# Routing counts in a fused attention, MLP and expert kernel: indicators in blocks of six token tiles, and two token tiles to one counting product in the six-bit rounds

## The chip, the cores and the metric

One core of a Trainium2 chip runs the whole program. The metric is the device time of one execution in microseconds; the time before is the median of three runs, 1070.74 us (1070.49 to 1074.46).

## The reference, cut to what matters

Chunked attention and an MLP produce one row of 512 numbers for each of 3072 tokens. The last part routes these rows to eight experts with a capacity of 384 tokens each, in the order of all 24576 logits, and sends each token through its expert:

```python
def _moe2_ref(x, w_gate, w1, w2) -> np.ndarray:
    N, D = x.shape
    E = w_gate.shape[1]
    cap = N // E
    logits = x @ w_gate
    flat = logits.flatten()
    order = np.argsort(-flat)
    ...
    for idx in order:
        tok, e = (int(idx) // E, int(idx) % E)
        if assigned[tok] >= 0 or counts[e] >= cap:
            continue
        assigned[tok] = e
        counts[e] += 1
    ...
    for e in range(E):
        mask = assigned == e
        h = np.maximum(x[mask] @ w1[e], 0.0)
        out[mask] = h @ w2[e]
    return out.astype(np.float32)
```

## The kernel before, in words

**Tokens and phases.** The 3072 tokens are 24 tiles of 128 (`T = 24`). The greedy assignment is done in eight phases: each phase finds the logit at which the next expert is full, assigns what lies above it, closes that expert and starts again. `route(ph)` (L810) does a phase. What it finds, `eid[ph]` (which expert) and `ids[ph]` (its 384 tokens, made in `listing`, L906), lets the expert's weights be fetched (`fetch`, L950) and its token rows be gathered (`gather`, L991).

**The search for the threshold.** A token's best logit is turned into an integer key of 32 bits, and the threshold is found digit by digit, from the top, in five rounds: `RB = ((25, 7), (18, 7), (12, 6), (6, 6), (0, 6))`, two rounds with digits of seven bits (128 values) and three with six bits (64 values). In a round VectorE builds indicators (`indicate`, L737): for each token and each digit value n, whether the token's digit is at least n, in bf16, in two buffers of 12 token tiles each (`NH = 2`, `HT = 12`). A token tile's 128 columns of digit values stand 12 elements apart, since the buffer is ordered by digit value and then by tile; the rounds of six bits fill 64 of the 128 columns. TensorE counts (L829 to L832): one product `first` times `q2` puts in the starting counts, and then there is one product for each of the 24 tiles, which loads the tile's 128 indicator columns as weights and streams the 8 columns of `oh` (which expert each token wants):

```python
pc = psa[0].tile([P, E], F32, tag="pa", name=f"pc{ph}_{r}")
matmul(0.05, pc, first, q2, start=True, stop=False)
for t in range(T):
    matmul(0.047, pc, ind[t // HT][:, :, t % HT], oh[:, :, t], start=False, stop=(t == T - 1))
```

VectorE reads the counts `pc` with a scan (L835), TensorE turns the result into the digit in one product `pb` (L838), and VectorE subtracts it from all keys (L843) before the next round's indicators. A phase thus has five round trips between VectorE and TensorE; the last phase needs none. That makes 35 rounds, 14 with seven bits and 21 with six.

**What runs beside it.** Phase 0 is routed at the end of the MLP: TensorE fills its pauses with products that were kept back for it, the late products (`late_`, L358, lines 346). When the last of them is done, VectorE makes the last tile of token rows (`finish`, L371 to L373) and GpSimd stores it; the gather of phase 0 on GpSimd's queue stands behind that store. Phases 1 to 6 are routed while TensorE runs the experts of the phase before: `ffn1` (products `pf`, 96 of 384 columns) and `ffn2` (products `pg`, 72 of 512 columns). The expert weights land in a ring of four buffers, ScalarE rounds each piece (`e_0`), and VectorE subtracts to get the remainder (`e_1`, in `second`, L972), after which the ring buffer takes the next piece.

**What sets the order.** PE, VectorE and ScalarE run in the order in which the Python code emits the instructions. A planner (`run`, L776) emits them: each piece of work is a generator that yields the engine it wants, a due time and a rank, `clk` holds the time that the planner books for each engine, and the products of `experts()` or `late()` fill TensorE until a piece falls due. A lower rank goes first on an engine: the chain of routing has rank 0 for counts and digits, its VectorE work rank 1 in phases 0 and 1 and rank 3 later, and `second` rank 2 from the third half-expert on.

**Names in the rows.** Buffers of the attention are used again: `vw` holds indicators, `kwin`, `qk`, `wk` and `kT` hold keys, masks and small tables, `o` is a late product's output, `x` a tile of token rows, `x2d` their store in memory, `xg` the gathered rows, `px` their transposes, `xgh` and `xgl` the two parts of these, `raws` the ring. All VectorE calls of the router have line 582 and all its products line 761, since helpers emit them.

## Time and profile before

| what | before |
|---|---|
| median of three runs | 1070.74 us |
| profiled execution: its time, its span | 1072.39 us, 1070.6 us |
| TensorE busy (matmul), share of the span | 1010.0 us, 94% |
| VectorE busy, share | 793.8 us, 74% |
| ScalarE busy, share | 460.7 us, 43% |
| GpSimd busy, share | 204.7 us, 19% |
| counting products with indicator weights (`pc`) | 840, 204 ns each from start to end |
| mean granted TensorE clock | 0.984 of full |

Busy time of TensorE counts from a product's start to its modelled end, and products overlap: the counting products are 204 ns long but start closer together than that. So a stage in which TensorE shows no idle time is read by the starts of its products and not by its busy share. The profile's slices show four stages: attention and MLP to about 683 us, the routing of phase 0 under the late products to 716 us, a gap with little on TensorE to about 735 us, and eight experts to the end.

### The profile page before, as it was taken

The numbers are of one execution on the slowest core, as the hardware profiler recorded it, in microseconds if no ns is written. First come the engines' busy times: TensorE is split into PE (matmuls) and PEld (weight loads), VectorE is DVE, ScalarE is ACT, GpSimd is POOL, SyncE is SP. The second block draws the span as 40 slices with busy tenths as digits, with TensorE's granted clock in tenths as the row PEclk, the third lists the DMA queues.
The fourth block names the chain that finished last, engine by engine and source line by source line (L and its number), as shares of the span: only waits on it lengthen the run. The fifth ranks groups of instructions, "written<-read, shape, count | busy, mean of one in ns | idle before, by whom it ended". The sixth has DMA issues, their size and how long they took to land.

```text
span 1070.6 us, 24583 instructions
## 1 busy us (share of the span) xinstructions
PE 1010.0 (94%) x9397; PEld 888.7 (83%) x9397; DVE 793.8 (74%) x2879; ACT 460.7 (43%) x991; POOL 204.7 (19%) x227
## 2 busy tenths in 40 slices
PE   4668899999999999999999999987999999999997
PEld 3647688888988889888888889866898988988996
DVE  4999864986698969898969854376968769678720
ACT  3666554444444544445444445312414334233621
POOL 2566540000021101021101000001103202032211
PEclk9989999999999999999999999996999999999999
DMA  6966504221212121212121100032624426235600
GB/s 158 230 184 185 148 19 128 58 58 38 58 38 59 39 58 38 57 39 59 38 58 39 38 2 2 20 117 91 197 92 145 130 88 208 88 140 176 227 30 30
DMA packets 140373, 96.52 MB, mean 90 GB/s; under 512 B 99288, under 2 KB 123864, under 8 KB 140128
## 3 DMA queue, kind: packets, MB, share of 16 engines
q1 hardware_dynamic: 135968, 81.32, 27.1%
q0 software_dynamic: 4000, 13.11, 3.4%
q8 instruction: 74, 1.21, 0.5%
q10 hardware_dynamic: 288, 0.52, 0.1%
q14 instruction: 43, 0.35, 0.1%
HBM read 82.33 MB, written 12.60 MB: 89 GB/s over the span
## 4 chain that ended last, share of the span: by engine, by line
PE 72%; DVE 14%; issue 6%; DMA 4%; ACT 1%; POOL 1%; SPq 1%; POOLq 0%; DVEq 0%; ACTq 0%
PE o L346 20%; PE ph L316 20%; PE pf L761 11%; PE pg L761 9%; DVE lsc L387 5%; PE pc L761 5%; DVE u L280 2%; DVE y L281 1%; DVE g L325 1%; PE po L221 1%; DMA xg<-x2d,vw 1%; PE sc L195 1%; PE px L1014 1%; DMA raw<-in_moe_w_out_dram 1%; DMA k<-in_k_dram 1%
## 5 line engine op out<-in xcount | busy, mean ns | idle before, releaser
L316 PE MATMUL ph<-xT,win 128*128 128x256 f32 x2304 | 321.9, 288 | 9.7 <-ACT win L262 6.9
L316 PEld LDWEIGHTS ph<-xT,win 128*128 128x128 f32 x2304 | 300.0, 192 | 27.5 <-ACT win L262 10.3
L346 PE MATMUL o<-wout,g 128*128 128x512 f32 x1038 | 275.3, 401 | 5.2 <-DVE g L325 2.2
L346 PEld LDWEIGHTS o<-wout,g 128*128 128x128 f32 x1038 | 185.1, 190 | 39.7 <-DVE g L325 3.1
L387 DVE SCALAR_TENSOR_TENSOR lsc<-x,wgb 128x128 int8<-128x128 f32 x640 | 158.2, 298 | 3.3 <-DMA wgb<-wgd 1.2
L320 ACT ACTIVATE r<-ph 128x256 f32<-128x256 f32 x192 | 72.7, 381 | 166.5 <-PE ph L316 155.8
L761 PE MATMUL pf<-xgh,e 128*128 128x384 f32 x512 | 137.9, 345 | 0.0
L761 PE MATMUL pg<-e,hh 128*128 128x512 f32 x384 | 124.3, 399 | 0.0
L325 DVE TENSOR_TENSOR g<-r,g 128x256 fp32r<-128x256 f32 x173 | 80.7, 468 | 53.3 <-ACT g L324 50.5
L387 DVE SCALAR_TENSOR_TENSOR lsc<-c,wgb 128x512 int8<-128x512 f32 x128 | 99.1, 774 | 2.1
L761 PEld LDWEIGHTS pf<-xgh,e 128*128 128x128 f32 x512 | 94.0, 192 | 0.4 <-ACT xgh L765 0.2
L761 PE MATMUL pf<-xgl,e 128*128 128x384 f32 x256 | 88.3, 345 | 0.3 <-DVE xgl L582 0.3
L765 ACT ACTIVATE hh<-pf 128x384 fp32r<-128x384 f32 x64 | 31.5, 492 | 129.1 <-PE pf L761 87.0
L765 ACT ACTIVATE e<-raws 128x1024 fp32r<-128x1024 f32 x64 | 65.7, 1056 | 45.5 <-DMA raws<-in_moe_w_dram 45.4
L321 ACT ACTIVATE r<-r 128x256 f32<-128x256 f32 x192 | 79.6, 417 | 5.5
L761 PEld LDWEIGHTS pg<-e,hh 128*128 128x128 f32 x384 | 71.1, 189 | 12.5
L582 DVE TENSOR_TENSOR e<-raws,e 128x1024 fp32r<-128x1024 f32 x64 | 76.8, 1218 | 3.9 <-ACT e L765 3.0
L761 PE MATMUL pg<-e,hl 128*128 128x512 f32 x192 | 75.8, 395 | 0.0
L324 ACT ACTIVATE g<-r 128x256 fp32r<-128x256 f32 x173 | 71.7, 417 | 5.0 <-PE o L346 0.3
L994 POOL DMA_INDIRECT xg<-x2d,vw x24 | 34.8, 1451 | 151.8 <-issue 118.2
L761 PE MATMUL pc<-kwin,vw 128*128 128x8 bf16 x840 | 56.2, 204 | 7.3 <-DVE vw L582 7.3
L582 DVE SCALAR_TENSOR_TENSOR hl<-pf,hh 128x384 fp32r<-128x384 f32 x64 | 35.1, 551 | 35.6 <-ACT hh L765 35.6
(171 smaller groups left out, 1276.7 us busy)
## 6 DMA issues: line engine op xcount, KB each, us to landing
raws<-in_moe_w_dram SPq DMA_DIRECT2D x64, 512.0 KB
vw<-in_v_dram SPq DMA_DIRECT2D x176, 56.0 KB
raw<-in_moe_w_in_dram SPq DMA_DIRECT2D x16, 512.0 KB
raw<-in_moe_w_out_dram SPq DMA_DIRECT2D x16, 512.0 KB
k<-in_k_dram SPq DMA_DIRECT2D x24, 256.0 KB
q<-in_q_dram SPq DMA_DIRECT2D x24, 256.0 KB
x2d<-x SPq DMA_DIRECT2D x20, 256.0 KB
wgb<-wgd SPq DMA_DIRECT2D x1, 2048.0 KB
```

The source lines that it names most:

```text
L280: nc.vector.scalar_tensor_tensor(u, yi, 3, u, op0=ALU.logical_shift_left, op1=ALU.bitwise_or)
L316: nc.tensor.matmul(ph, win_ap(a, kk, f), x[:, kk, :], start=(n == 0), stop=(n == 3 * KD - 1))
L320: nc.scalar.activation(r, ph, AF.Relu)
L321: nc.scalar.activation(r, r, AF.Square)
L324: nc.scalar.activation(hi, r, AF.Copy)
L325: nc.vector.tensor_tensor(lo, r, hi.bitcast(F32), op=ALU.subtract)
L346: nc.tensor.matmul(PO[j][u], g[:, u * P:(u + 1) * P], wout_ap(a, f), start=(f == 0 and n == 0), stop=(f == FT - 1 and n == 2))
L387: nc.vector.scalar_tensor_tensor(sc[:, z], a[:, z], 1.0, b[:, z], op0=ALU.mult, op1=ALU.mult, accum_out=acc[:, i:i + 1])
L582: return getattr(nc.vector, name)(out, *args, **kw)
L761: return nc.tensor.matmul(*args, **kw)
L765: nc.scalar.activation(out, in_, func)
L994: nc.gpsimd.indirect_dma_start(out=xg[:, j, :], out_offset=None, in_=x2d[:, :], in_offset=bass.IndirectOffsetOnAxis(ap=ids[ph][:, j:j + 1] ...
```

## The change

**Layout.** An indicator buffer is ordered by block of six token tiles, then digit value, then tile in the block (`blocks`). A tile's columns then stand 6 elements apart instead of 12, and in a round of six bits the 64 columns of a tile in one block and the 64 columns of the tile in the next block lie at one step behind each other.

**Counting.** In the rounds of six bits one product takes both: 128 weight columns of two tiles against 16 columns, the 8 of `oh` for each. Of the four quarters of its output two mean something: digit values of the first tile with its own 8 columns (partitions 0 to 63, columns 0 to 7), and those of the second (partitions 64 to 127, columns 8 to 15). VectorE copies the second quarter to partitions 0 to 63, adds the first, and scans the sum on 64 partitions; `pb` is made from 64 partitions. A round of six bits has 13 products instead of 25; a round of seven bits keeps its 25.

**VectorE's pieces.** In phases 0 and 1 each block's indicators are an instruction of their own, four to a round instead of two. The remainders of the first three half-experts are made in half pieces (`second`). **Ranks and due times.** VectorE's routing work from phase 2 on has rank 2 instead of 3, and the counting products of a six-bit round fall due 0.3 us later against the indicators than those of a seven-bit round.

```diff
-    q2 = b0.tile([P, E], BF16, name="q2")
+    q2 = b0.tile([P, 2 * E], BF16, name="q2")
...
     def indicators(n):
-        return [sp.tile([P, P, HT], BF16, tag=f"ind{g}", name=f"ind{n}_{g}") for g in range(NH)]
+        return [sp.tile([P, HT // TB, P * TB], BF16, tag=f"ind{g}", name=f"ind{n}_{g}")
+                .rearrange("p k m -> p (k m)") for g in range(NH)]
+
+    def blocks(ind, n):
+        return ind[:, :HT * n].rearrange("p (k n b) -> p k n b", n=n, b=TB)
...
     def indicate(ind, de, g, r):
-        n, z = 2 ** RB[r][1], [P, 2 ** RB[r][1], HT // TB, TB]
-        V.tensor_tensor(ind[:, :n, :].rearrange("p n (a b) -> p n a b", b=TB),
-                        de[:, g * HT:(g + 1) * HT].rearrange("p (a b) -> p a b", b=TB)[:, None].to_broadcast(z),
-                        tabs[r][:, :, None, :].to_broadcast(z), op=ALU.is_ge)
+        n, k = 2 ** RB[r][1], HT // TB
+        z = [P, k, n, TB]
+        V.tensor_tensor(blocks(ind, n),
+                        de[:, g * HT:(g + 1) * HT].rearrange("p (a b) -> p a b", b=TB)[:, :, None, :].to_broadcast(z),
+                        tabs[r][:, None, :, :].to_broadcast(z), op=ALU.is_ge)
...
-        rank = 1 if ph < 2 else 3
+        rank = 1 if ph < 2 else 2
...
-                    indicate(ind[g], de, g, r)
-                yield "pe", V_PE - 0.5 + sl, 0
-                pc = psa[0].tile([P, E], F32, tag="pa", name=f"pc{ph}_{r}")
-                matmul(0.05, pc, first, q2, start=True, stop=False)
-                for t in range(T):
-                    matmul(0.047, pc, ind[t // HT][:, :, t % HT], oh[:, :, t], start=False, stop=(t == T - 1))
+                    if ph > 1:
+                        indicate(ind[g], de, g, r)
+                    else:
+                        n = 2 ** RB[r][1]
+                        for k in range(HT // TB):
+                            V.tensor_tensor(blocks(ind[g], n)[:, k], de[:, None, g * HT + k * TB:g * HT + (k + 1) * TB]
+                                            .to_broadcast([P, n, TB]), tabs[r], op=ALU.is_ge)
+                yield "pe", V_PE - (0.5 if RB[r][1] == 7 else 0.2) + sl, 0
+                n = 2 ** RB[r][1]
+                k = P // n
+                pc = psa[0].tile([P, k * E], F32, tag="pa", name=f"pc{ph}_{r}")
+                matmul(0.05, pc, first, q2[:, 0:k * E], start=True, stop=False)
+                for g in range(T // (k * TB)):
+                    x = ind[g * k * TB // HT].rearrange("p (m b) -> p m b", b=TB)[:, g * k * TB % HT // TB * n:, :]
+                    y = oh[:, :, g * k * TB:(g + 1) * k * TB].rearrange("p e (k b) -> p b k e", b=TB)
+                    for b in range(TB):
+                        matmul(0.047, pc, x[:, 0:P, b], y[:, b], start=False, stop=(g + 1) * k * TB + b == T + TB - 1)
                 yield "v", PE_V, 0
                 fl = small([P, E], BF16, "fl")
-                V.tensor_tensor_scan(fl, pc, ones[:, 0:E], 0.0, op0=ALU.max, op1=ALU.min)
+                if k > 1:
+                    ab = small([P, E], F32, "ab")
+                    V.tensor_copy(ab[0:n], pc[n:P, E:2 * E])
+                    V.tensor_tensor(ab[0:n], pc[0:n, 0:E], ab[0:n], op=ALU.add)
+                V.tensor_tensor_scan(fl[0:n], ab[0:n] if k > 1 else pc, ones[0:n, 0:E], 0.0, op0=ALU.max, op1=ALU.min)
                 yield "pe", V_PE + sl / 2, 0
                 pb = psa[0].tile([P, 2], F32, tag="pa", name=f"pb{ph}_{r}")
-                matmul(0.05, pb, steps[r], fl[:, E - 2:E], start=True, stop=True)
+                matmul(0.05, pb, steps[r][0:n], fl[0:n, E - 2:E], start=True, stop=True)
...
         def second(hi, lo, raw):
-            yield "v", A_V, rank
-            V.tensor_tensor(lo, raw, hi.bitcast(F32), op=ALU.subtract)
+            m = raw.shape[1]
+            k = m // 2 if h < 3 else m
+            for z in range(0, m, k):
+                yield "v", A_V if z == 0 else 0.0, rank
+                V.tensor_tensor(lo[:, z:z + k], raw[:, z:z + k], hi[:, z:z + k].bitcast(F32), op=ALU.subtract)
```

**What it moves.** The planner's times change, so the order of all three engines changes from the routing of phase 0 on. On TensorE, at the end of phase 0's routing, before (`pi` makes the token list of phase 0, `o` are late products, `kT` is the weight of the first counting product of phase 1):

```order
L761 MATMUL pi_10270<-rounded 128x26 x3
L346 MATMUL o_1_9965<-wout_81,k_9785 128x512
L346 MATMUL o_1_9965<-wout_79,k_9785 128x512 x2
L346 MATMUL o_1_9965<-wout_81,k_9785 128x512
L346 MATMUL o_1_9965<-wout_79,k_9785 128x512 x2
L346 MATMUL o_1_9965<-wout_81,k_9785 128x512
L346 MATMUL o_1_9965<-wout_79,k_9785 128x512 x2
L346 MATMUL o_1_9965<-wout_81,k_9785 128x512
L346 MATMUL o_1_9965<-wout_79,k_9785 128x512 x2
L346 MATMUL o_1_9965<-wout_81,k_9785 128x512
L346 MATMUL o_1_9965<-wout_79,k_9785 128x512
L761 LDWEIGHTS kT_9685
```

With the change, the same stretch:

```order
L767 MATMUL pi_10258<-rounded 128x26 x3
L346 MATMUL o_1_9965<-wout_79,k_9785 128x512 x2
L346 MATMUL o_1_9965<-wout_81,k_9785 128x512
L346 MATMUL o_1_9965<-wout_79,k_9785 128x512
L767 LDWEIGHTS kT_9685
```

Behind `pi` stood 14 late products (a row with x2 is two), and 4 stand there now; the ten others have gone in front of it, between the rounds of phase 0.

On VectorE, a little later, before (`x_23` is the last tile of token rows, `kwin_0` and `vw_0` keys and indicators of phase 1):

```order
L582 TENSOR_TENSOR kwin_0_9681<-kwin_0_9681,kT_9685 128x120
L582 TENSOR_TENSOR vw_0_9679<-kwin_0_9681,qk_9684 128x24
L582 TENSOR_TENSOR vw_0_9679<-vw_0_9679,kT_9686 128x1536
L373 SCALAR_TENSOR_TENSOR x_23_10303<-o_1_9965,s_col,wsum 128x512
L582 TENSOR_TENSOR e_1_10227<-raws,e_0_10226 128x4x256
```

And with the change (`kwin_0<-L` is the start of phase 1's routing):

```order
L582 TENSOR_TENSOR kwin_0_9681<-L,qk_9684 128x192
L582 TENSOR_REDUCE wk_9688<-kwin_0_9681 128x24
L373 SCALAR_TENSOR_TENSOR x_23_10271<-o_1_9965,s_col,wsum 128x512
L582 TENSOR_TENSOR kwin_0_9681<-kwin_0_9681,wk_9688 128x192
L582 TENSOR_TENSOR kwin_0_9681<-kwin_0_9681,kT_9685 128x192
```

The last tile of token rows stood behind phase 1's first indicators (`128x1536`); it now stands nine instructions earlier, behind the second instruction of phase 1.

On VectorE in phase 1, with the change, from the digit of round 1 to the counts of round 2, the first round of six bits (`xgl` is the second part of the gathered rows, `e_1` the remainder of expert 0's second weights):

```order
L582 SCALAR_TENSOR_TENSOR vw_0_9679<-kwin_0_9681,pb_1_10400 128x24
L582 TENSOR_TENSOR vw_0_9679<-vw_0_9679,kT_9685 128x384 x2
L582 TENSOR_TENSOR xgl_10348<-px_0_10349,xgh_10347 128x384
L582 TENSOR_TENSOR xgl_10348<-px_1_10350,xgh_10347 128x384
L582 TENSOR_TENSOR xgl_10348<-px_2_10351,xgh_10347 128x384
L582 TENSOR_TENSOR xgl_10348<-px_3_10352,xgh_10347 128x384
L582 TENSOR_TENSOR e_1_10393<-raws,e_0_10392 128x512
L582 TENSOR_TENSOR vw_0_9680<-vw_0_9679,kT_9685 128x384 x2
L582 TENSOR_TENSOR e_1_10393<-raws,e_0_10392 128x512 x2
L582 COPY wk_9688<-pc_2_10427 64x8
L582 TENSOR_TENSOR wk_9688<-pc_2_10427,wk_9688 64x8
L582 SCALAR_TENSOR_TENSOR kT_9685<-wk_9688,kT_9685 64x8
```

Before, the four `xgl` stood behind the indicators and counts of round 2, with whole pieces of `e_1` (128x1024) among them. Now they stand between the two halves of that round's indicators, and the counts are followed by a copy, an addition and the scan.

## Rows read from the trace of the kernel before

**Rows 1.** Windows of the whole program: engine busy time, granted clock, DMA share, GB/s.

```profile
710.00:720.00 10.00, 6.72 (x40) 5.39 (x38) 8.85 (x23) 4.24 (x4) 0.57 (x1) 0.94 0.60 203
720.00:740.00 20.00, 11.73 (x108) 10.08 (x109) 15.10 (x25) 5.88 (x8) 5.14 (x3) 0.50 0.46 152
...
740.00:980.00 240.00, 240.00 (x1721) 213.47 (x1721) 186.14 (x458) 81.55 (x125) 40.59 (x30) 0.99 0.39 130
```

**Rows 2.** The page's chain that ended last, by engine.

```profile
PE 72%; DVE 14%; issue 6%; DMA 4%; ACT 1%; POOL 1%; SPq 1%; POOLq 0%; DVEq 0%; ACTq 0%
```

**Rows 3.** Timeline of one six-bit round among expert products (start, length, engine, instruction).

```profile
872.89 0.34 PE L761 MATMUL pf<-xgl,e 128*128 128x384 f32 x1
873.07 0.18 PE L761 MATMUL pc<-qk,kT 128*128 128x8 bf16 x1
873.11 1.58 PE L761 MATMUL pc<-kwin,vw 128*128 128x8 bf16 x24
...
874.54 0.60 PE L761 MATMUL pf<-xgh,e 128*128 128x384 f32 x2
...
874.72 0.17 DVE L582 TENSOR_TENSOR_SCAN kT<-pc,kT 128x8 bf16<-128x8 f32 x1 [1.34 <-PE pc L761]
...
875.32 0.18 PE L761 MATMUL pb<-kT,wk 128*128 128x2 bf16 x1
```

**Rows 4.** Chain of waits from 680 us on: the expert products of phase 7.

```profile
996.29 16.67 PE pf L761 x96
```

**Rows 5.** Windows around twelve counting products each, at either clock.

```profile
717.65:718.55 0.90, 0.90 (x12) 0.81 (x12) 0.90 (x2) 0.29 (x1) 0.00 (x0) 1.00 0.00 0
...
723.81:724.70 0.89, 0.89 (x12) 0.80 (x12) 0.89 (x1) 0.78 (x1) 0.89 (x1) 0.50 1.07 324
```

**Rows 6.** Weight loads by shape: bf16 loads of indicators and of contiguous tiles.

```profile
L761 PEld LDWEIGHTS <-vw 128*128 128x128 bf16 x840 | 53.7, 162 | 7.8 <-DVE vw L582 7.7
L761 PEld LDWEIGHTS <-kT 128*128 128x128 bf16 x70 | 6.5, 100 | 12.7 <-issue 12.6
```

**Rows 7.** Timeline: three bf16 products with contiguous weights, first and last.

```profile
882.60 0.18 PE L761 MATMUL pt<-wk,kT 128*128 128x8 bf16 x1
...
882.66 0.17 PE L761 MATMUL pt<-vw,qk 128*128 128x8 bf16 x1
```

**Rows 8.** Timeline at the end of the late products.

```profile
712.10 0.40 PE L761 MATMUL pi<-rounded 128*128 128x26 f32 x3
712.35 3.44 PE L346 MATMUL o<-wout,k 128*128 128x512 f32 x14
...
713.53 0.62 DVE L582 TENSOR_REDUCE wk<-kwin 128x24 f32<-128x192 f32 x1
...
717.51 0.74 DVE L373 SCALAR_TENSOR_TENSOR x<-o,s_col,wsum 128x512 f32<-128x512 f32 x1
...
718.57 0.57 POOL L374 DMA_DIRECT2D x2d<-x  x1 [12.20 <-DVE x L373]
...
721.96 1.53 POOL L994 DMA_INDIRECT xg<-x2d,vw  x1 [2.82 <-PE pb L761]
...
734.96 0.69 PE L761 MATMUL pf<-xgh,e 128*128 128x384 f32 x1
```

**Rows 9.** VectorE by shape from 740 us on (busy us, mean ns | idle before).

```profile
L582 DVE TENSOR_TENSOR e<-raws,e 128x1024 fp32r<-128x1024 f32 x56 | 67.1, 1218 | 3.7 <-ACT e L765 2.8 <-PE pf L761 0.9
...
L582 DVE TENSOR_TENSOR vw<-vw,wk 128x768 bf16<-128x768 bf16 x12 | 6.3, 554 | 0.2
L582 DVE TENSOR_TENSOR vw<-kwin,kT 128x1536 bf16<-128x1536 bf16 x6 | 5.7, 953 | 0.1
...
L582 DVE TENSOR_TENSOR vw<-vw,pt 128x8 f32<-128x8 f32 x12 | 1.9, 158 | 0.2
```

**Rows 10.** Waits from 740 us on: VectorE's scan waiting for the counts.

```profile
DVE kT L582 <- PE pc L761: 24.9, 25, 2.1
```

**Rows 11.** Timeline: a counting product of phase 1 that waits for indicators.

```profile
738.08 1.63 PE L761 MATMUL pc<-kwin,vw 128*128 128x8 bf16 x24 [0.46 <-DVE vw L582]
```

More of the change, by code (lines that the diff above doesn't have):

```diff
@@ L663, in start_counts @@
     def start_counts():
-        V.tensor_scalar(q2[0:1], q[0:1], -256.0, None, op0=ALU.max)
-        V.tensor_scalar(q2[32:33], q[32:33], 256.0, 0.0, op0=ALU.add, op1=ALU.min)
+        V.tensor_scalar(q2[0:1, 0:E], q[0:1], -256.0, None, op0=ALU.max)
+        V.tensor_scalar(q2[32:33, 0:E], q[32:33], 256.0, 0.0, op0=ALU.add, op1=ALU.min)
     start_counts()
@@ L725, in prep @@
             V.tensor_tensor(ez, dz[:, 0, :], act[:, t0:t1], op=ALU.min)
-            if ph == 0:
-                for a in range(t0 - t0 % TB, t1, TB):
-                    g, a, b = a // HT, max(a, t0), min(a + TB, t1)
-                    V.tensor_tensor(ind[g][:, :2 ** RB[0][1], a - g * HT:b - g * HT],
-                                    de[:, None, a:b].to_broadcast([P, 2 ** RB[0][1], b - a]),
-                                    tabs[0][:, :, a % TB:a % TB + b - a], op=ALU.is_ge)
-            for g in range(NH) if ph else ():
+            for a in range(t0 - t0 % TB, t1, TB) if ph < 2 else ():
+                if ph and a:
+                    yield
+                a, b = max(a, t0), min(a - a % TB + TB, t1)
+                V.tensor_tensor(blocks(ind[a // HT], 2 ** RB[0][1])[:, a % HT // TB, :, a % TB:a % TB + b - a],
+                                de[:, None, a:b].to_broadcast([P, 2 ** RB[0][1], b - a]),
+                                tabs[0][:, :, a % TB:a % TB + b - a], op=ALU.is_ge)
+            for g in range(NH) if ph > 1 else ():
                 if g:
```

## The prediction

> **What bounds the kernel now.** I read the windows first. From 740 to 980 us, phases 0 to 5 of the experts, TensorE is busy for all 240 us and VectorE for 186 [rows 1]. Before that lies a gap: from 720 to 740 us TensorE has 11.7 of 20 us at the lower of its two clocks (granted 0.50, 1.2 GHz), and from 710 to 720 us 6.7 of 10. The chain that ended last says the same of the whole: 72% of it is TensorE, 14% VectorE [rows 2]. So a product that goes from the expert stage is worth its spacing, and in the gap the chain from the last late product to the first expert product counts. The timeline shows the spacing. In a six-bit round of phase 4 the last expert product in front of the counts starts at 872.89, 25 counting products follow, the next expert product starts at 874.54 [rows 3]. An expert product of 384 columns takes 16.67/96 = 0.174 us [rows 4], so the 25 took 1.48 us. The expert product behind them shows 0.09 us more than usual (0.60 for two, where 0.51 is 0.17 + 0.34), so 1.48 to 1.57 us, 0.059 to 0.063 each; I use 0.061.
>
> What sets this 0.061? Twelve products take 0.90 us at granted clock 1.00 and 0.89 us at 0.50 [rows 5], so it is not the array's clock. The weights do: a load of an indicator tile, columns 24 bytes apart, takes 162 ns, one of a contiguous bf16 tile 100 ns [rows 6], and three products with contiguous weights start within 0.06 us, 0.03 apart [rows 7]. So the spacing is that of reading strided weights, and the 8 columns streamed are hidden under it.
>
> **Part 1, half the products in six-bit rounds.** 12 fewer products in each of 21 rounds. The 18 rounds of phases 1 to 6 lie among expert products: 18 x 12 x 0.061 = 13.2 us. The 8 further columns of each product cost at most 8 x 0.174/384 = 0.004 us each, 0.05 us a round, if the load did not cover them, and nothing if it does. I take nothing, since the half clock did not show them either; 18 x 0.05 = 0.8 us stays in the range.
>
> **Part 2, the shorter step.** The columns now stand 12 bytes apart in all 35 rounds. No row shows such a load. Bounds: the 24-byte one, 0.061 a product, and the contiguous one, 0.03. In phases 1 to 6, 12 x 24 + 18 x 12 = 504 indicator products remain, so this is worth between 0 and 504 x 0.031 = 15.6 us. I take 0, as the 24-byte row is the nearer: neighbouring columns are still never side by side. A load that gets slower is excluded, since the step only shrinks.
>
> The Trainium skill, TensorE: Matmul & The Clock Gate, section LDWEIGHTS, makes a load's time a matter of its column count alone, 128/1.2 = 107 ns by its formula, whatever the step. The trace does not agree (162 and 100 ns for the same 128 columns [rows 6]); by that rule part 2 would be 0.
>
> **Part 3, copy, addition and scan.** A six-bit round gets two more VectorE instructions in its chain. Neither is in the trace; the nearest row is an 8-column operation on counts in PSUM, 158 ns [rows 9], with some 0.04 us between dependent ones: 0.4 us for the two. Bounds: nothing, if they run while TensorE has other products; 0.4 a round, if TensorE waits for them. In phases 1 to 6 I take nothing. Today the scan starts at 874.72 and ends at 874.89, and `pb`, which needs it, runs at 875.32: 0.43 us spare [rows 3]. In the new order 6 or 7 expert products stand between the counts and `pb` from phase 2 on, against 4, which gives another 0.35 us or more. VectorE has the time: it has waited 24.9 us in 25 scans, 1 us each, for the counts [rows 10]. Without that cover the cost is 18 x 0.4 = 7.2 us; behind the scan are the next round's indicators, for which the next counts would then wait.
>
> **Part 4, the end of phase 0.** Three six-bit rounds of phase 0 lie among late products, 36 products or 2.2 us. The planner fills the room: ten late products go in front of `pi`, 10 x 3.44/14 = 2.4 us [rows 8]. So `pi` (712.10) comes at about the same time, 0.2 us later, but 4 late products follow it and not 14. They ended at 715.8; they will end at 712.35 + 0.2 + 4 x 0.24 = 713.5. The last token tile on VectorE started only at 717.51, behind phase 1's first indicators [rows 8]. Now it stands behind the reduction that ended at 714.15, so it starts at 714.3: 3.2 us earlier. The store (718.57) and the gather behind it (721.96) [rows 8] follow on GpSimd's queue with nothing in between, as do the gather's landing, the transposes and the first expert product, now at 734.96. I take the full 3.2 us; the bounds are 3.2 and 0 (the next late thing would be phase 1's indicators, which the first counting products among the transposes need).
>
> **Part 5, VectorE's smaller pieces.** An instruction more costs its fixed part: 2 x 554 - 953 = 155 ns, from one of 1536 elements against two of 768 [rows 9]. In phase 0 this goes into `pi`'s chain, where the planner's late products cover it. After the gather, phase 1 gets 10 more indicator instructions and expert 0 and 1 twelve more remainders, 3.4 us. Some of it meets TensorE: in the new order all four `xgl` and a half remainder stand between the two halves of round 2's indicators, 4 x 0.5 + 0.7 = 2.7 us, and the counts of that round stand behind only seven expert products, 7 x 0.174 to 7 x 0.35 us (1.2 to 2.4) by the clock. TensorE already waits at such a place, 0.46 us at 738.08 [rows 11]. I take 2.4 us lost. Bounds: 0, since 36 expert products stand between the counts of rounds 2 and 3 and let VectorE catch up, and all 3.4.
>
> Phases 2 to 6 keep their two indicator instructions a round. The rank changes put routing level with the remainders there; the cover is VectorE's 54 idle us of 240 [rows 1], and without it a late weight would stop TensorE once a phase.
>
> **Sum.** 13.2 + 3.2 - 2.4 = 14.0 us off the profiled execution's 1072.39 us (span 1070.6), 1058.4. That execution is 1.65 us above the median of the runs, so against the median 1070.74 - 14.0 = **1056.7 us**.
>
> **Rivals.** *Shorter step, quicker loads.* If the time of a load goes with how often a read leaves the 16 bytes it has just touched, 4 columns touch 3 stretches instead of 4. Then 0.061 becomes 0.046, and 504 x 0.015 = 7.6 us more come off: 1049. For it: the spacing does not move with the clock and halves without a step [rows 5 to 7]; against it: no row lies between the two steps. Chance 0.25.
>
> The Trainium skill, SBUF — State Buffer, section Door 1: The DMA port swizzle, says that accesses within one 16-byte line run at full bandwidth and each step to a new line pays; by that rule this rival is the forecast, and the rows at 24 bytes and at none agree with it.
>
> *VectorE takes it back.* The longer chain (part 3 without cover, 7.2 us) makes TensorE wait before `pb` in each six-bit round: 1064. For it: VectorE works in order, and remainders of 1.22 us [rows 9] can stand in front of a copy; against it: the 1 us waits of [rows 10]. Chance 0.15, a third of it within 0.5% of no change.
>
> *Slower: the copy between partitions.* It reads partitions 64 to 127 and writes 0 to 63, which no row here shows. The pair has 0.43 + 0.35 us spare and may use up 0.73 us of saved products and 0.05 of part 4's gain (0.8 over 18 rounds) before the kernel loses: it decides at about 1.6 us a pair, four times my price. At 2.2 us the rounds lose 18 x (2.2 - 0.78 - 0.73) = 12.4 us, less the 0.8: 1082. Against it: the nearest small operation takes 0.158 us [rows 9]. Chance 0.03.
>
> *It does not do what it says.* If a product over 16 columns with weights from two blocks takes twice as long, the rounds save nothing, and with 0.8 us from phase 0 it is 1070. The 0.004 us a column-octet speaks against it. Chance 0.04.
>
> **How the numbers follow.** Forecast 0.53, then 0.25, 0.15, 0.03, 0.04. A measurement of this kernel can tell about 0.5% from no change, 5.4 us, so faster means below 1065.4: 0.53 + 0.25 + 0.10 = 0.88. Same: 0.05 + 0.04 = 0.09. Slower: 0.03. The forecast's own range is 1053 (nothing lost in part 5, a little from part 2) to 1061 (no gain in part 4, 0.8 us of part 1's columns). The range reaches below to 1048, which takes in the quicker loads at three stretches in four but not the contiguous bound (1041), and above to 1063, which takes in half of VectorE's case.
>
> **What would show it.** Counting products in the expert stage fall from 25 to 13 in a six-bit round and the round from 1.5 us to 0.8. Their spacing stays at 0.061; 0.046 or a load well below 162 ns makes the first rival right. `x` of the last tile starts at about 714.3, the first gather near 718.8, the first `pf` near 732. TensorE shows no wait for the scan between 740 and 980 us. From a `pf` to the same `pf` of the next phase the time shrinks by 3 x 0.73 = 2.2 us. If it shrinks by less than 0.6, or copy and addition take more than 0.8 us together, I am wrong.

## The result and the profile after

The changed kernel takes **1055.97 us** (median of 3 runs, 1055.40 to 1056.12), the kernel before 1070.74: a ratio of **0.9847** (95% interval 0.9824 to 0.9870). The two medians lie 14.8 us apart; the ratio makes it 16.4 us. The forecast was 1056.7. The profiled execution has a span of 1054.4 us against 1070.6, so 16.2 us have to be found in its rows. The total came out as forecast; most of its terms did not.

The windows of the changed kernel, in the columns of [rows 1]:

```profile
710.00:720.00 10.00, 3.90 (x36) 2.99 (x36) 9.02 (x23) 4.02 (x4) 3.12 (x3) 0.76 0.55 161
720.00:740.00 20.00, 16.35 (x101) 14.12 (x99) 16.25 (x40) 7.00 (x11) 1.34 (x1) 0.61 0.39 139
740.00:980.00 240.00, 237.67 (x1583) 204.82 (x1582) 204.57 (x527) 88.24 (x133) 43.00 (x36) 0.99 0.44 145
```

The gap ahead of the experts is shorter, VectorE has gone from 186 to 205 busy us of 240, and TensorE, which had no idle time there, now has 2.3 us of it. The chain that ended last is still TensorE's:

```profile
PE 70%; DVE 15%; issue 8%; DMA 3%; ACT 2%; POOL 1%; SPq 0%; POOLq 0%; DVEq 0%; ACTq 0%
```

One six-bit round of an undisturbed phase, from the timeline (start, length, engine, instruction), as in [rows 3]:

```profile
860.63 0.34 PE L767 MATMUL pf<-xgh,e 128*128 128x384 f32 x1
860.81 0.18 PE L767 MATMUL pc<-qk,kT 128*128 128x16 bf16 x1
860.85 0.71 PE L767 MATMUL pc<-kwin,vw 128*128 128x16 bf16 x12
861.41 0.42 PE L767 MATMUL pf<-xgh,e 128*128 128x384 f32 x1
861.60 0.17 DVE L582 COPY wk<-pc 64x8 f32<-64x8 f32 x1 [0.49 <-PE pc L767]
...
861.80 0.16 DVE L582 TENSOR_TENSOR wk<-pc,wk 64x8 f32<-64x8 f32 x1
...
861.99 0.17 DVE L582 TENSOR_TENSOR_SCAN kT<-wk,kT 64x8 bf16<-64x8 f32 x1
...
862.38 0.34 PE L767 MATMUL pf<-xgh,e 128*128 128x384 f32 x1
862.65 0.17 PE L767 MATMUL pb<-kT 64*128 64x2 bf16 x1
862.76 0.45 PE L767 MATMUL pf<-xgh,e 128*128 128x384 f32 x1
863.04 0.34 PE L767 MATMUL pf<-xgl,e 128*128 128x384 f32 x1
```

From the start of the expert product ahead of the counts to that of the next are 0.78 us; less its own 0.174 that leaves 0.61 us for 13 counting products, where 25 took 1.48 [rows 3]. That is 0.047 us each, not 0.061. Copy and addition put the scan 0.39 us later (861.60 to 861.99), as priced. Two things are new: the shorter spacing, and `pb`. On its 64 rows `pb` starts 0.27 us behind the expert product in front of it and lets the next one start only 0.38 us after that product's start.

The weight loads by shape give the reason for the spacing: an indicator tile with columns 12 bytes apart loads in 142 ns, not 162 [rows 6]; contiguous tiles still take 100.

```profile
L767 PEld LDWEIGHTS <-vw 128*128 128x128 bf16 x588 | 30.8, 142 | 7.4 <-DVE vw L582 7.3
L767 PEld LDWEIGHTS <-kT 128*128 128x128 bf16 x63 | 5.7, 100 | 11.6 <-issue 11.5 <-DVE hl L582 0.2
```

Windows around 12 and around 24 such products, the second at the lower clock level (granted 0.50, 1.2 GHz), show that the clock has no part in it (the instruction counts take in neighbours at the window's edge). With 0.17 to 0.2 us for the last product's own length, both come to 0.046 to 0.049 us a product:

```profile
860.85:861.56 0.71, 0.71 (x15) 0.71 (x15) 0.26 (x1) 0.00 (x0) 0.71 (x1) 1.00 0.00 0
725.09:726.34 1.25, 1.25 (x27) 1.25 (x26) 0.00 (x0) 0.00 (x0) 0.00 (x0) 0.50 0.95 351
```

The end of phase 0, to be read against [rows 8]:

```profile
684.40 0.18 PE L767 MATMUL pc<-qk,kT 128*128 128x8 bf16 x1
...
710.72 0.40 PE L767 MATMUL pi<-rounded 128*128 128x26 f32 x3
710.97 1.17 PE L346 MATMUL o<-wout,k 128*128 128x512 f32 x4
...
712.68 0.74 DVE L373 SCALAR_TENSOR_TENSOR x<-o,s_col,wsum 128x512 f32<-128x512 f32 x1
...
713.74 0.57 POOL L374 DMA_DIRECT2D x2d<-x  x1 [12.42 <-DVE kwin L582]
...
717.07 1.23 POOL L1018 DMA_INDIRECT xg<-x2d,vw  x1 [2.76 <-DMA x2d<-x]
...
727.23 0.69 PE L767 MATMUL pf<-xgh,e 128*128 128x384 f32 x1
```

The order is as read from the change: four late products behind `pi`, `x` behind one reduction. The first counting product of phase 0 stood at 685.31 before:

```profile
685.31 0.18 PE L761 MATMUL pc<-qk,kT 128*128 128x8 bf16 x1
```

The gains against before grow along the chain: the first counting product 0.9 us, `pi` 1.4, `x` 4.8, the first gather 4.9, the first expert product **7.7 us**.

From there on I count by phases: a phase lasts from its first `pf` to the first `pf` of the next, both read from the timeline. Before: 47.17, 42.12, 43.60, 43.60, 43.60, 41.08, 34.40 us. After: 45.25, 41.64, **45.10**, 40.95, 40.95, 38.76, 34.38. So 7.7 + 1.9 + 0.5 - 1.5 + 2.65 + 2.65 + 2.3 = 16.2 us. Phase 2 is the odd one: 4.15 us longer than the two behind it, longer even than before. (A phase is undisturbed when TensorE waits for nothing in it: phases 3 and 4 here, phases 2 to 4 before.) TensorE's waits around its start, from the timeline:

```profile
811.29 0.33 PE L1038 MATMUL px<-ident,xg 128*128 128x128 f32 x1 [0.58 <-DMA xg<-x2d,vw]
...
815.49 0.45 PE L767 MATMUL pf<-xgl,e 128*128 128x384 f32 x1 [0.42 <-DVE xgl L582]
...
816.71 0.44 PE L767 MATMUL pf<-xgl,e 128*128 128x384 f32 x1 [0.42 <-DVE xgl L582]
...
818.77 0.45 PE L767 MATMUL pc<-kwin,vw 128*128 128x16 bf16 x6 [0.79 <-DVE vw L582]
```

Behind these waits the clock falls. From 821 to 824 us the granted clock is 0.50, the lower of its two levels (1.2 GHz). In the windows it is the third column from the right:

```profile
818.00:820.00 2.00, 1.23 (x11) 1.23 (x12) 1.97 (x4) 0.46 (x1) 0.00 (x0) 1.00 0.00 0
820.00:822.00 2.00, 1.88 (x9) 1.54 (x8) 1.90 (x7) 0.03 (x1) 0.00 (x0) 0.74 0.00 0
...
821.00:824.00 3.00, 3.00 (x11) 3.00 (x10) 1.59 (x4) 0.49 (x1) 0.00 (x0) 0.50 0.00 0
...
822.00:826.00 4.00, 4.00 (x27) 3.63 (x26) 1.17 (x5) 0.49 (x1) 0.00 (x0) 0.71 0.00 0
```

Waits of 1.63 us inside the phase, and 2 x 0.26 + 4 x 0.29 = 1.7 us of lost clock, make 3.3 of the 4.15. (The 1.7 is an estimate, as if all products went by the clock.) The first thing late is the token list of phase 2, on VectorE:

```profile
797.43 0.62 DVE L582 SCALAR_TENSOR_TENSOR rounded<-qk,rounded,kwin 128x384 fp32r<-128x384 f32 x1
797.97 0.35 DVE L582 TENSOR_TENSOR kwin<-L,qk 128x192 f32<-128x192 f32 x1
...
800.51 0.23 DVE L582 TENSOR_TENSOR kwin<-pi,qk 128x72 f32<-128x72 f32 x1
...
801.97 0.98 POOL L1018 DMA_INDIRECT xg<-x2d,vw  x1 [1.76 <-issue]
```

`pi` ran at 798.76, but six instructions of phase 3's preparation (from 797.97) stand ahead of the comparison that reads it. The gather goes out 29.5 us behind the first `pf` of phase 1 (772.48), under which phase 2 is routed; in the undisturbed phases it goes out 24.8 us behind (859.22 to 883.98).

### The profile page after: what moved, and what is told of

It is laid out like the page before. It is cut to its first block, busy times and chain, and to the rows that moved or that the text cites. A ratio compares the mean times of both kernels' runs of the same rounds, so it can differ in the third digit from the quotient of the medians.

```text
span 1054.4 us, 24153 instructions
## 1 busy us (share of the span) xinstructions
PE 994.1 (94%) x9145; PEld 868.1 (82%) x9145; DVE 801.4 (76%) x2951; ACT 460.7 (44%) x991; POOL 199.5 (19%) x227
## 4 chain that ended last, share of the span: by engine, by line
PE 70%; DVE 15%; issue 8%; DMA 3%; ACT 2%; POOL 1%; SPq 0%; POOLq 0%; DVEq 0%; ACTq 0%
PE ph L316 20%; PE o L346 20%; PE pf L767 12%; PE pg L767 9%; DVE lsc L387 5%; DVE u L280 2%; PE pc L767 2%; DVE y L281 1%; DVE g L325 1%; PE po L221 1%; PE sc L195 1%; DMA xg<-x2d,vw 1%; PE px L1038 1%; DMA raw<-in_moe_w_in_dram 1%; DVE u L278 1%
## 5 line engine op out<-in xcount | busy, mean ns | idle before, releaser
L582 DVE TENSOR_TENSOR e<-raws,e 128x1024 fp32r<-128x1024 f32 (+1 forms) x76 | 78.8, 1051 | 3.8 <-ACT e L771 2.9
L1018 POOL DMA_INDIRECT xg<-x2d,vw x24 | 28.0, 1167 | 144.6 <-issue 79.8
L1111 POOL DMA_INDIRECT out_dram<-qk,vw x24 | 29.2, 1215 | 133.3 <-ACT qk L771 104.2
```

The lines of the kernel that those rows point to most:

```text
L582: return getattr(nc.vector, name)(out, *args, **kw)
L1018: nc.gpsimd.indirect_dma_start(out=xg[:, j, :], out_offset=None, in_=x2d[:, :], in_offset=bass.IndirectOffsetOnAxis(ap=ids[ph][:, j:j + 1] ...
L1111: st_ = nc.gpsimd.indirect_dma_start(out=out[:, :], out_offset=bass.IndirectOffsetOnAxis(ap=ids[ph][:, j:j + 1], axis=0), in_=o, in_offset ...
```

## The experiments

Twelve runs, in three groups. Each is given as a ratio to the kernel before, timed beside it in the same group (medians of before 1072.65, 1072.31, 1072.25 us). Each diff shows the lines that matter most.

**e1_blocks: the shorter step alone.** The kernel before with blocks of six token tiles; nothing paired, 24 products in each round.

```diff
-  matmul(0.047, pc, ind[t // HT][:, :, t % HT], oh[:, :, t], ...)
+  x = ind[t // HT].rearrange("p (m b) -> p m b", b=TB)[:, t % HT // TB * n:, :]
+  matmul(0.047, pc, x[:, 0:P, t % TB], oh[:, :, t], ...)
```

> The kernel before with the indicators in blocks of six token tiles alone: every round keeps its 24 products, all VectorE pieces, ranks and due times stay. Theory A (the step of the weight load counts: 12 bytes take 142 ns where 24 bytes took 162, and products follow each other in 0.046 instead of 0.061 us): 30 rounds x 24 products of phases 1 to 6 x 0.015 = 10.8 us, and some 84 products of phase 0 x 0.015 = 1.3, together 12 us: about 1058.5 us, first to next counting product 0.046 us in every round, a six-bit round still 24 products in about 1.1 us. Theory B (the gain of the change came from fewer products alone, and the shorter step is an effect of the pairs): no change, 1069.5 to 1071 us, spacing 0.061.

Ratio **0.9901** (0.9884 to 0.9919), 1061.7 us, 10.6 us less. Theory A holds. The load takes 143 ns in its trace, and the undisturbed phase falls from 43.60 to 41.97 us: 1.63, where 120 products x 0.015 make 1.8. The step that the prediction priced at nothing is worth 1% by itself.

**e2_pair24: the pairs alone, at the old step.** Both halves of the token tiles in one buffer, columns 0 to 63 and 64 to 127, 12 products of 24-byte step. Copy, addition and `pb` are as in the change; VectorE's pieces, ranks and due times are as before.

```diff
-  indicate(ind[g], de, g, r)
+  indicate(ind[g] if RB[r][1] == 7 else ind[0][:, g * 64:(g + 1) * 64, :], de, g, r)
```

> The kernel before with the pairs alone, at the old step: six-bit rounds put both halves of the token tiles into one indicator buffer (columns 0 to 63 and 64 to 127, step 24 bytes), 12 products instead of 24, copy, add, scan and pb on 64 rows as in the change; VectorE pieces, ranks and due times as before. Theory A: spacing 0.061 us, 216 products x 0.061 = 13.2 us less, phase 0's end about 3 us earlier (10 late products fewer), and 18 pb products on 64 rows give back 0.18 each = 3.2 us: about 1057.5 us. Theory C (a pb on 64 rows costs nothing, its gap in the changed kernel has another cause): about 1054.3 us. If nothing of a saved product arrives at the end: 1068 to 1071 us.

Ratio **1.0006** (0.9997 to 1.0015): nothing arrives. Neither theory had this; the third reading comes nearest. 252 products are gone, the first expert product comes 2.3 us earlier and phase 0 is 4.5 us shorter (42.65), and then phases 2 to 5 of 44.2, 45.9, 44.1 and 44.2 us lose it all. Their timeline shows waits for the gather (1.16 us), `xgl` (0.48, 1.49) and indicators (1.25 twice), as in phase 2 of the changed kernel, at the starts of phases 3 and 5. In phase 4 it shows hardly one: 114 counting products run there and 64 in phase 3, where an undisturbed phase has 89, so rounds have slipped over the border and the two lengths are to be read together.

**e3_pb128: pb on all 128 rows.** The changed kernel; rows 64 to 127 of the steps are zero.

```diff
-  matmul(0.05, pb, steps[r][0:n], fl[0:n, E - 2:E], start=True, stop=True)
+  matmul(0.05, pb, steps[r], fl[:, E - 2:E], start=True, stop=True)
```

> The changed kernel with one edit: in six-bit rounds pb takes all 128 rows again (rows 64 to 127 of the steps are zero, those of fl are left from a seven-bit round), instead of 64. Theory A (a product on 64 rows between products on 128 rows stops the next loads and costs 0.31 us instead of 0.13): 18 x 0.18 = 3.2 us less, about 1052.8 us, and pf to pf across pb 0.13 us above a plain pf step. Rival (the gap at pb has another cause, such as the due time): 1055.5 to 1056.5 us, the gap stays at 0.31.

Ratio **0.9812** (0.9797 to 0.9828), 1052.4 us. Theory A holds. Its timeline:

```profile
859.01 0.34 PE L767 MATMUL pf<-xgh,e 128*128 128x384 f32 x1
859.19 0.18 PE L767 MATMUL pb<-kT 128*128 128x2 bf16 x1
859.23 0.42 PE L767 MATMUL pf<-xgh,e 128*128 128x384 f32 x1
859.49 0.34 PE L767 MATMUL pf<-xgl,e 128*128 128x384 f32 x1
```

From the product ahead of `pb` to the second behind it are 0.48 us, where the changed kernel has 0.66 (862.38 to 863.04): 0.18 us for each `pb`. The undisturbed phase falls from 40.95 to 40.44 us, 0.51 for three. The Trainium skill, TensorEngine Tiling (Array Packing), section Key Properties, says that going from one tiling mode of the array to another drains it. That fits the 0.18 us here, but what TensorE does in that time no run shows.

One thing more sets this trace apart. The waits at the start of phase 2 are the same as in the change, but the clock does not fall behind them (waits, then the window):

```profile
814.09 0.44 PE L767 MATMUL pf<-xgl,e 128*128 128x384 f32 x1 [0.42 <-DVE xgl L582]
...
815.30 0.45 PE L767 MATMUL pf<-xgl,e 128*128 128x384 f32 x1 [0.43 <-DVE xgl L582]
...
817.37 0.45 PE L767 MATMUL pc<-kwin,vw 128*128 128x16 bf16 x6 [0.79 <-DVE vw L582]
...
812.00:826.00 14.00, 12.25 (x98) 10.49 (x97) 11.26 (x27) 4.86 (x9) 0.62 (x1) 1.00 0.09 35
```

Its phase 2 takes 43.1 us, 2.0 less than in the change, where `pb` accounts for 0.5. So some 1.5 us of e3's gain in the profiled spans (4.9 us) go with the clock, and `pb`'s price is the 0.51 us a phase.

**e4_whole and e6_rank3: VectorE's part undone, whole and the rank alone.** e4 takes back the smaller pieces and the rank, e6 the rank alone (its edit):

```diff
-  rank = 1 if ph < 2 else 2
+  rank = 1 if ph < 2 else 3
```

> The changed kernel with VectorE's part undone: indicators of phase 1 (and of phase 0's later rounds) a half at a time, the subtractions of the first three weight halves whole, and rank 3 instead of 2 for the routing from phase 2 on. Blocks, pairs and due times stay. Theory of the prediction (the smaller pieces free xgl and pc earlier at the start): about 2.4 us slower, 1058.4 us, with waits for xgl near 730 us. Rival D (they buy nothing at the start, and rank 2 makes the list of phase 2 late, which costs phase 2 some 4 us): 1052 to 1055 us, phase 2 from first pf to first pf 41 us instead of 45.1.

> The changed kernel with rank 3 instead of 2 for the routing from phase 2 on, and nothing else: smaller pieces stay. Theory F (the rank is what lets the shorter phases stay without waits: with rank 3 the routing falls behind the weights' subtractions and every second gather is late): phases of 43.6 and 45 us in turn as in e4, 1063 to 1067 us, ratio 0.992 to 0.995. Rival (the smaller pieces carry it): 1056 us, ratio 0.985, phases of 40.95 us.

e4: **0.9949** (0.9931 to 0.9967); e6: **0.9971** (0.9957 to 0.9985). Both readings of e4 failed: it neither loses 2.4 us nor gains, it loses some 11. (The first reading also turns the prediction round, in which the smaller pieces cost 2.4 us; the same holds for the rival in e9.) e6 settles where: the rank. Without it some 3 of the 16.4 us are left. Its phases 1 to 4 take 46.5, 45.5, 43.9 and 45.2 us; the gather for phase 4 and the waits around that phase's start, from its timelines:

```profile
893.36 0.98 POOL L1018 DMA_INDIRECT xg<-x2d,vw  x1 [1.64 <-issue]
...
903.38 0.33 PE L1038 MATMUL px<-ident,xg 128*128 128x128 f32 x1 [1.38 <-DMA xg<-x2d,vw]
...
909.77 0.44 PE L767 MATMUL pf<-xgl,e 128*128 128x384 f32 x1 [1.49 <-DVE xgl L582]
```

The gather goes out 30.75 us behind the first `pf` of phase 3 (862.61). In e6 and in e4 the starts of phases 2, 4 and 6 have such waits (in e6 that of phase 1 too), and those of phases 3 and 5 have none. That a phase long by waits gives the next list room would explain it, but no run shows it. Behind the waits the clock falls here too (granted 0.50, 1.2 GHz, from 823 to 828 and from 911 to 917 us).

**e5_early2: phase 2's routing ahead as well.** e3 with one more edit:

```diff
-  rank = 1 if ph < 2 else 2
+  rank = 1 if ph < 3 else 2
```

> The kernel with pb on 128 rows (e3) and rank 1 instead of 2 for the routing of phase 2 as well (rank 1 below phase 3). Theory E (phase 2 is long in the changed kernel, 45.1 us, because its list is late on VectorE: the first gather is issued 29 us after the first pf of the phase before, and 24.8 us in the later phases): the gather comes at most 27 us after that pf, TensorE waits for neither px nor xgl there, the phase takes 40.5 us instead of 43.1, ratio to the kernel before 0.979 (e3 had 0.9812), about 1050 us. Rival (VectorE is full there, and what the routing gains the weights' subtractions lose): a wait for e in place of it, ratio 0.981 or above.

Ratio **0.9762** (0.9742 to 0.9782), **1047.2 us**, the fastest kernel of the study, 25 us below the one before. The gather goes out 23.6 us behind the first `pf` of phase 1 (771.84 to 795.42); phases 1 to 4 take 39.67, 40.45, 40.45 and 40.44 us, and from phase 1 on the timeline shows no wait on TensorE at all. Theory E holds, and the gain is larger than it said. (Its edits together with the larger pieces of e9, below, were not run.)

**e7_pair24_rank2: the pairs at the old step, with rank 2** and `pb` on 128 rows (e2 with two edits).

> The pairs at the old step (e2) with rank 2 for the routing from phase 2 on and pb on 128 rows. Theory F and the prediction's price (a saved product is worth 0.061 us at 24 bytes, and e2 lost it to late gathers): steady phases of 43.6 - 36 x 0.061 = 41.4 us without waits, 1055 to 1058 us, ratio 0.985 to 0.988. Rival (pairs at the long step save nothing, or late gathers come from elsewhere): phases of 44 us, 1069 to 1073 us, ratio 0.998 or above.

Ratio **0.9845** (0.9825 to 0.9864), phases 2 to 4 of 41.42, 41.45 and 41.45 us without waits. Theory F holds: 43.60 - 41.45 = 2.15 us against 36 x 0.061 = 2.2. From e2 to e7 the ratio falls by 0.0161, 17 us; some 3 of them are `pb`'s rows by the 0.51 us a phase of e3. So e2 lost most of its gain to the order on VectorE, and not to the products.

**e9_bigger: the larger pieces back, rank 2 kept.** e4 with the rank of the change.

> The changed kernel with VectorE's larger pieces back (indicators of phase 1 and of phase 0's later rounds a half at a time, subtractions of the first three weight halves whole), rank 2 kept. Theory F (rank 2 alone carries VectorE's part): ratio 0.983 to 0.987 as the change, steady phases 40.95 us. Rival (the prediction's price: the pieces are worth 2.4 us at the first expert's start): ratio 0.987 to 0.990, with the loss ahead of the second pf phase.

Ratio **0.9793** (0.9777 to 0.9810), 1050.4 us: faster than the change by 0.0054 of 1071, 5.8 us. Neither reading had this. The first expert product comes 1.5 us later than in the change (728.69), phase 0 is 1.5 us shorter, so the smaller pieces buy nothing at the start; and phase 2 takes 40.93 us, not 45.10. In its timeline the list is on time:

```profile
795.19 0.62 DVE L582 SCALAR_TENSOR_TENSOR rounded<-qk,rounded,kwin 128x384 fp32r<-128x384 f32 x1
...
797.11 0.22 DVE L582 TENSOR_TENSOR kwin<-pi,qk 128x72 f32<-128x72 f32 x1
...
798.56 0.98 POOL L1018 DMA_INDIRECT xg<-x2d,vw  x1 [23.70 <-PE pg L767]
```

The routing is 2.2 us further (795.19 against 797.43 at nearly the same first `pf`, 772.47 and 772.48), the comparison follows 1.9 us after it and not 3.1, and the gather goes out at 26.1 us, not 29.5. The undisturbed phase is the same with either (40.95 us), so what costs is how the pieces shift the order that the planner lays down for phase 1. With rank 3 they cost less, 2.4 us by the ratios of e4 and e6, whose intervals overlap.

**e10_before_rank2: the rank alone,** in the kernel before.

> The kernel before with rank 2 instead of 3 for the routing from phase 2 on, and nothing else. Theory F (the rank buys time only where shorter phases make the gather late; before had no wait between 740 and 1070 us): no change, ratio 0.997 to 1.002, phases 43.6 us, gathers earlier in the phase. Rival (rank 2 is worth time by itself, or makes the weights late): ratio outside 0.995 to 1.005.

Ratio **1.0002** (0.9988 to 1.0016): nothing, as theory F has it. The rank earns nothing; it keeps what shorter phases earn.

This trace tells something else as well. Up to 757 us its engines run the same instructions in the same order as before, and yet the first gather and the first expert product come earlier, 721.36 and 733.05 where before had 721.96 and 734.96 [rows 8]:

```profile
721.36 1.53 POOL L994 DMA_INDIRECT xg<-x2d,vw  x1 [2.82 <-PE pb L761]
...
733.05 0.69 PE L761 MATMUL pf<-xgh,e 128*128 128x384 f32 x1
```

So the place of the first `pf` differs by 1.9 us between two executions of one order.

**e11_due: the due time back to 0.5 us.**

> The changed kernel with the due time of the six-bit rounds' products back at 0.5 us ahead of VectorE's end (0.2 in the change). Theory H (13 products take 0.6 us instead of 1.5, so the second half's indicators are wanted sooner; 0.3 us too early makes TensorE wait in the three six-bit rounds of each phase): a wait of pc for VectorE of up to 0.3 us a round, 0 to 5 us in all, ratio 0.985 to 0.990. Rival (VectorE has slack there): no wait, ratio 0.983 to 0.986.

Ratio 0.9853 (0.9835 to 0.9871), not to be told from the change's 0.9847, and within both ranges. The long phases are others (46.7, 47.1, then 41.0), no wait for indicators shows in the undisturbed ones, and they take 41.0 to 41.1 us instead of 40.95. At most 0.15 us a phase; the rest stays open.

**e8_step6 and e12_early2_step6: an even shorter step.** e3 and e5 with `TB = HT // 4`, blocks of three token tiles, columns 6 bytes apart.

> The kernel with pb on 128 rows (e3) with blocks of three token tiles instead of six: the columns of a weight load are 6 bytes apart. Theory G (the load's time falls with the bytes between its columns: 162 ns at 24, 142 at 12, 100 in one piece): load near 120 ns, spacing 0.035 to 0.040 us, 84 products of a steady phase x 0.008 = 0.7 us less a phase, ratio 0.977 to 0.979. Rival (VectorE pays for runs of three elements, or the load gains nothing below 12 bytes): spacing 0.046, or VectorE's indicator pieces dearer than 554 and 953 ns with new waits, ratio 0.981 or above.

> Early routing of phase 2 (e5) with blocks of three token tiles (step 6 bytes). Theory (e8 lost its time in phase 2 alone, 46.9 us, to the late list; its later phases were 40.4 us): phase 2 at 40.4 us or a little more, ratio 0.976 to 0.978, level with e5, since the dearer indicator pieces (692 and 1225 ns instead of 554 and 954) make TensorE wait 0.6 us a phase for what the loads gain. Rival (VectorE too full at 6 bytes also with the early list): ratio 0.980 or above.

e8: **0.9841** (0.9819 to 0.9862), slower than e3 by 0.0029, where the intervals just overlap. e12: **0.9833** (0.9814 to 0.9852), clearly slower than e5. The load does gain, as the groups of e8's weight loads say (x294 of the 588 each):

```profile
L767 PEld LDWEIGHTS <-vw 128*128 128x128 bf16 x294 | 11.3, 104 | 6.2 <-DVE vw L582 5.9
L767 PEld LDWEIGHTS <-kwin 128*128 128x128 bf16 x294 | 11.1, 105 | 0.1
```

104 ns is a contiguous tile's time, less than the 120 expected, and 12 products start within 0.37 us, 0.031 each. But VectorE pays, in its groups by shape:

```profile
L582 DVE TENSOR_TENSOR kwin<-wk,kT 128x1536 bf16<-128x1536 bf16 x10 | 12.2, 1225 | 0.3
...
L582 DVE TENSOR_TENSOR kwin<-wk,kT 128x768 bf16<-128x768 bf16 x10 | 6.9, 692 | 0.3
```

A piece of 1536 elements takes 1225 ns instead of 953, and of 768 692 instead of 554 [rows 9]. The counts now wait for indicators in every phase, so the undisturbed phase stays at 40.4 us, and phase 1 (e8, 46.9 us; the expectation of e12 calls it phase 2 by mistake) or phase 0 (e12, 46.0 us, with a first expert product only at 732.2) loses more, with waits for indicators, for the scan and, in e8, for `xgl`. Part of this is the clock: it is granted at 0.50 (1.2 GHz) from 776 to 785 us in e8 and from 777 to 783 us in e12. My expectation for e12, level with e5, was wrong: the earlier routing shortens phase 1 to 41.3 us, and phase 0 is longer by 2.8 than in e8. The rival had the ratio.

## Why the prediction was right, and where it was not

The undisturbed phase separates the products' terms, since nothing waits in it: 43.60 us before; 41.97 with the shorter step (e1); 40.45 with the pairs too (e5); 40.95 with `pb` on 64 rows (the change).

**Part 1, 13.2 us: right at its step.** At 24 bytes a saved product is worth what was forecast (e7). In the changed kernel the products that remain are cheaper and so were those saved: 41.97 - 40.45 = 1.52 us a phase, not 2.2.

**Part 2, taken as 0: the step that failed.** "I take 0, as the 24-byte row is the nearer: neighbouring columns are still never side by side." They don't have to be. The load took 142 ns and the product 0.047 us, against 0.046 in the first rival, which had a chance of 0.25. That one of the two rows lay nearer was no reason; they (162 and 100 ns) said only that the step matters. The three steps now give 162, 142 and 104 ns at 24, 12 and 6 bytes, and 100 in one piece. The Trainium skill, SBUF — State Buffer, section Door 1: The DMA port swizzle, asks for two or more accesses in each 16-byte line for full bandwidth. By an estimate from that page's 16 bytes there are 1.33 at a step of 12 bytes and 2.67 at 6, and the loads agree: 142 ns is between the extremes, 104 ns near the contiguous 100. This rule, cited beside that rival, was the better forecast. The rule that the prediction cites from the Trainium skill, TensorE: Matmul & The Clock Gate, section LDWEIGHTS, a time by the column count alone (107 ns), does not agree with the three times.

**Part 3, taken as 0: right for what it named.** The pair cost 0.39 us in VectorE's chain, and between 740 and 980 us TensorE has no wait for the scan beyond 0.12 us at 820.50, in the disturbed phase. But the same edit put `pb` on 64 rows, and that I did not price at all: 18 x 0.18 = 3.2 us by the timeline, 3.7 by the ratios of e3 and the change (0.0035 of 1071), with the clock of phase 2 in it.

**Part 4, 3.2 us: right for the order that it read; the rest of the 7.7 us is in part scatter and in part open.** The stretch from `pi` to `x` went from 5.4 to 2.0 us, 3.4 us shorter: four products behind `pi`, `x` behind the reduction. Ahead of it 1.4 us were gained and not 0.2 lost. Of these, 0.9 were there at the first counting product (685.31, now 684.40). That is no gain of the change: it is there already at 596 us, ahead of the first instruction that the change touches (the last one before it on VectorE starts at 596.04, now at 595.15), and in e10, with before's own order, the first counting product stands at 684.71. The other 0.5 lie between that product and `pi`. By an estimate from the runs, the 84 cheaper products of phase 0 give 84 x 0.014 = 1.2 us, three `pb` on 64 rows cost 0.5, and the forecast had 0.2 lost, which makes 0.5. Behind `x`, the stretch from the first gather to `pf` shrank by 2.8 us (13.0 to 10.2; the waits for the gather in it from 3.7 to 2.0). It is 11.7 us in e10, so 1.3 of the 2.8 come and go without any change. The seven kernels with pairs at 12 bytes have 10.2 to 11.1 us there, the seven others 11.7 to 14.1; no experiment says why. Each half of the change alone brings the first `pf` 2.7 us (e1) and 2.3 us (e7) forward, little more than e10's 1.9. e4, which has both halves without rank and smaller pieces, brings it 6.9 us forward (728.08), so rank and pieces have little part in it.

**Part 5, -2.4 us: right in sign, wrong in place and size.** The 2.4 was a choice between bounds of 0 and 3.4 and no sum. The pieces cost 5.8 us (e9; 4.9 by the spans), not at the first expert but mostly in phase 2, by a late list. And the rank, which got one sentence ("the cover is VectorE's 54 idle us of 240"), decides whether there is a gain: with rank 3 the ratio is 0.9971 (e6). The sentence looked for a late weight; what comes late is the list. VectorE's mean idle time says nothing on that: after the change VectorE idles 35 us of 240, and phases with one order have no waits and with another lose 4 us.

**Sum.** Two gains not seen (the step, and 4.5 us at the first `pf`, some of it scatter) stood against two losses not seen (`pb`, phase 2). That the forecast hit 1056 was luck, and the starting point had a part in it: the 14.0 us were taken off a median of three runs, 1070.74, where the later groups of 13 and 17 runs have 1072.25 to 1072.65. Against the 16.4 us of the ratio the forecast is 2.4 us short. The rival "VectorE takes it back" was nearer to the truth than its chance of 0.15: VectorE's order does take most of the gain back in e6 (0.9971), though by the late list and not by copy and scan.

## What to carry to other kernels

When an edit shortens the bounding engine, list what must now come earlier by the same amount, and look at its place in the order on the engine that makes it: here one planner rank was worth nothing before the change and 13 us after it. Price a change of layout on both sides of the buffer, by the reader's step and the writer's run: 12 bytes gained on TensorE without loss on VectorE (a piece of 1536 indicators still takes 954 ns in e1), 6 bytes gained more and lost it. Run the kernel before once more when the end of a phase is read from one trace: here its first expert product moved by 1.9 us without an edit. And run the parts of a change apart even when the total agrees: the fastest kernel here (1047.2 us) came from undoing one operand's rows and moving one rank.

## What was not expected of the hardware

- A bf16 weight load of 128 columns took 162, 142, 104 and 100 ns with columns 24, 12, 6 and 2 bytes apart, and small products followed each other in 0.061, 0.047, 0.031 and 0.03 us. At 24 and at 12 bytes this was the same at either clock.
- A product with 64 rows of weights among products with 128 cost 0.18 us more than one with 128, though it works on half the data; its own load is shorter (93 ns).
- VectorE wrote 1536 bf16 indicators in 953 ns when the innermost dimension of its operands had six elements, and in 1225 ns when it had three (e8).
- In the changed kernel waits of 0.42, 0.42 and 0.79 us at the start of phase 2 were followed by a granted clock of 0.50 (1.2 GHz) from 821 to 824 us, which cost about as much again as the waits. In e3 waits of 0.42, 0.43 and 0.79 us at the same place were not: the clock stayed at 1.00 (2.4 GHz).
